# Linear attention and a squared-ReLU block with fast matrix products: the last weight pieces asked for ahead of W_out's stores, and the opening's units in another order

## The chip, the cores and the metric

The kernel runs on one core of one Trainium2 chip. The metric is the device time in microseconds (us) of one execution. Before the change the median of three runs is 915.18 us (915.45, 915.18, 912.42). A core has five engines that work at the same time and wait for one another through semaphores: TensorE (PE, with its weight loads shown as PEld), VectorE (DVE), ScalarE (ACT), GpSimd (POOL), and SyncE (SP), which here only issues DMAs. Each engine takes its instructions in the order in which the program lists them.

## The reference

```python
def _attn_ref(q, k, v, g_norm):                 # (8, 8, 576, 64) each
    kv = np.einsum('bhsd,bhse->bhde', k, v)
    out = np.einsum('bhsd,bhde->bhse', q, kv)
    rms = np.sqrt(np.mean(out * out, axis=-1, keepdims=True) + 1e-06)
    return (out / rms * g_norm).astype(np.float32)

def _moe_ref(x, w_in, w_out):                   # (4608, 512), (512, 2048), (2048, 512)
    h = x @ w_in
    r = np.maximum(h, 0.0)
    g = r * r
    return (g @ w_out).astype(np.float32)

def reference(**kwargs):
    ...
    x = np.ascontiguousarray(attn_out.transpose(0, 2, 1, 3)).reshape(B * S, H * D)
    return _moe_ref(x=x, **moe_kwargs)
```

Attention without softmax: per batch and head a 64 x 64 matrix kv is summed over the sequence, the queries are multiplied with it, and each row of 64 is divided by its root mean square. The result, 4608 tokens of 512 features, goes through a feed-forward block of width 2048 whose activation is the square of ReLU. The two weight matrices arrive as 64-bit floats, which the kernel gets as pairs of 32-bit words.

## The kernel before

**Units and strips.** The work on queries, keys and values is cut into units (b, p): batch b and pair p of heads, of which there are four (NP) per batch. The feed-forward block works on nine strips of 512 tokens (N_STRIP). Its two products are computed by Strassen-like schemes: a product of 2 x 2 blocks is made of seven block products (ORDER = 1, 2, 6, 5, 7, 3, 4) on sums of blocks. The first strip (s = 0) is special: its up product is plain (`up_first`, L745), because the weights arrive only then, and its down product (`down`, L842) takes the seven blocks of W_out, in the order 1, 2, 5, 6, 7, 3, 4. Blocks 1, 2 and 5 lie in SBUF, in three parts of the tile `w_in` (`w_first`, L218); blocks 6, 7, 3 and 4 are fetched from the DRAM tile `w_out` by `stream` (L798) into tiles `w_blk`. Each block is also cut a second time: `deep_sums` (L885) makes four sums of its quarters in a tile `w_t`, and `store_deep_sums` (L828) stores them to `w_deep` for the later strips. `w_blk` and `w_t` share one pool of four buffers.

**Weight pieces.** Each matrix arrives in 16 pieces of 512 KB (`load_piece`, L227, into eight buffers `raw`); pieces 0 to 15 are W_in, 16 to 31 W_out. A piece is converted to 32-bit floats in two steps on ACT (`convert_on_act`, L238: tiles `w_c` and `raw`) and four on DVE (`conversion`, L248). `convert_pieces` (L265) does a pair of pieces, has ACT work up to two pieces ahead, and asks for further pieces at its end (`load_more`, L274). The second half of W_out's pieces (24 to 31) goes through `sums_out` (L300): conversion, block sums (L280), and four stores of 256 KB for each pair (L313). `store_first(b)` (L319, L321) stores one of the three parts kept in SBUF, in two DMAs of 512 KB.

**The order.** The whole order is written out by hand. The opening is the list `slices` from L623 to L628: T is `transposed_query` (four PE transposes and a copy on ACT), K is `key_value` (products of keys and values on PE, two copies into `kv_all` on ACT), Q is `first_queries` (products with the queries, then ACT's squares and DVE's means), N is `first_normalized` (a root on ACT, then DVE, tile `x_n`), F is `first_features` (transposes of x_n on PE, copy on ACT), `act` and `piece` are the steps of a conversion on ACT and on DVE, and U is `first_up`, the first products of the up part. `keep_busy(ps, n)` (L360) lets PE multiply the identity matrix n times into a PSUM tile that is overwritten later.

After the opening, the loop at L1189 goes through the steps i of strip 0: 16 steps of `up_first` (n_up = 16) and 14 of `down`. Around each step stand the calls of `convert`, which emit the conversions; `attend`, which emits the next entries of `slices` (units of batch 1, then the features of strip 1); and the loads. Units are loaded in a fixed order by `load_next` (L174): it is called with steps 0, 1 and n_up + 8, and after the keys of units (1, 0) and (1, 1), which asks for (1, 3) and (2, 0):

```python
            if b < 2:
                if b == 1 and p < 2:
                    load_next()
```

All these DMAs, stores too, are issued by SP and so stand in one queue, in the order in which the program lists them.

Of the kernel before, what the change touches and what calls it, by code (L numbers as in the profile page):

```python
# [10 lines left out]
FP32 = mybir.dt.float32  # L11
# [9 lines left out]
def kernel(  # L21
# [35 lines left out]
    P = 128  # L57
# [6 lines left out]
    C = S // P  # L64
# [4 lines left out]
    NT = 4  # L69
# [104 lines left out]
    def load_next(q_eng=nc.sync, names="kvq"):  # L174
        u = next(to_load, None)
        if u is not None:
            load(*u, q_eng, names)
# [141 lines left out]
    def store_first(b):  # L319
        for e in range(2):  # L320
            nc.sync.dma_start(out=w_out[b, :, e], in_=w_first[b][:, :, ts(e, P)])  # L321
# [38 lines left out]
    def keep_busy(ps, n):  # L360


        for _ in range(n):
            nc.tensor.matmul(ps, lhsT=ident, rhs=ident[:, : ps.shape[1]], start=True, stop=True)
# [34 lines left out]
    def key_value(b, *ps_of):  # L399
        while any(f == load and a[:2] == (b, p) or f == load_rest and a[0] == b for _, f, a in keys_due for p in ps_of):  # L400
            _, f, a = keys_due.popleft()
            f(*a)
        ps = apsum.tile([P, len(ps_of), D], FP32, name="kv_ps", tag="at")
        for i, p in enumerate(ps_of):
            tk, tv = main.pop(("k", b, p)), main.pop(("v", b, p))
            if (b, p) == (0, 0):
                keep_busy(ps[:, 0], 3)
            half = slice(REST * (b % 2), REST * (b % 2 + 1))
            for c in range(C + 1):
                for h in range(2):  # L410
                    a, w = (t[:, h, c, :] if c < C else r[half, 2 * p + h] for t, r in ((tk, k_rest), (tv, v_rest)))
                    nc.tensor.matmul(ps[ts(h, D), i], lhsT=a, rhs=w, start=c == 0, stop=c == C)  # L412
        at = (NP * b + ps_of[0]) % (2 * NP)
        d = kv_all[:, at : at + len(ps_of)]
        nc.scalar.copy(d[0:D, :, 0:D], ps[0:D])
        nc.scalar.copy(d[D:P, :, D:P], ps[D:P])
        for i, p in enumerate(ps_of):
            kvd[b, p] = d[:, i]
            if b < 2:
                if b == 1 and p < 2:  # L420
                    load_next()
            else:
                u = next(to_load, None)
                if u is not None:
                    keys_later(load, *u, nc.sync, "kv")
                if p == NP - 1 and b + 1 < B:
                    keys_later(load_rest, b + 1, nc.sync)
# [88 lines left out]
    first = {}  # L516
# [100 lines left out]
    slices, ready = [], {}  # L617
# [2 lines left out]
        convert_on_act, transposed_query, key_value, first_queries, first_normalized, first_features, first_piece  # L620
    )
    U = first_up
    slices += [(T, (0, 0)), (K, (0, 0)), (Q, (0,)), (T, (0, 1)), (K, (0, 1)), (N, (0,)), (Q, (1,)), (act, (0,))]  # L623
    slices += [(T, (0, 2)), (F, (0,)), (K, (0, 2)), (piece, (0, 2)), (N, (1,)), (Q, (2,)), (act, (1,)), (piece, (0, 2))]
    slices += [(T, (0, 3)), (F, (1,)), (K, (0, 3)), (U, (0, [0])), (piece, (1, 2)), (N, (2,)), (Q, (3,)), (act, (2,))]
    slices += [(piece, (1, 2)), (U, (0, [1, 2])), (piece, (2, 1)), (N, (3,)), (act, (3,)), (F, (2,)), (U, (1, [0]))]
    slices += [(piece, (2, 3)), (F, (3,)), (piece, (3, 4))]
    slices += [(U, (1, [1, 2])), (U, (2, [0, 1, 2])), (U, (3, [0, 1, 2]))]  # L628
    ready[0] = len(slices)
    def query_pairs(b):  # L630
# [534 lines left out]
    for s in range(N_STRIP):  # L1165
        attend(ready[s])
        if s == DEEP_UP - 1:
            while queried:
                attend(slice_at[0] + 1)
            psums.close()  # L1170
            fpsum = ctx.enter_context(tc.tile_pool(name="fpsum", bufs=5, space=bass.MemoryType.PSUM, reuse_waits="tile"))
            apsum = ctx.enter_context(tc.tile_pool(name="apsum", bufs=1, space=bass.MemoryType.PSUM, reuse_waits="tile"))
        if s >= DEEP_UP:
            steps = [(0.5, up_slot, (s, slot)) for slot in range(55)]
        elif s == 0:
            steps = [(2, up_first, (g, fh, i)) for g in range(NG) for fh in range(2) for i in range(2)]
        else:
            steps = [(1, up, (s, g, p)) for g in range(NG) for p in ORDER]
        n_up = len(steps)
        if s < DEEP:  # L1180

            steps += [(2, down, (s, p, i)) for p in (ORDER if s else (1, 2, 5, 6, 7, 3, 4)) for i in range(2)]
        else:
            steps += [(2, down_deep, (s, k, i)) for k in range(7) for i in range(2)]
        goal, begun = ready.get(s + 1, len(slices)), slice_at[0]
        if s >= DEEP_UP:
            goal = max(goal, min(ready[DEEP_UP] + (len(slices) - ready[DEEP_UP]) * (s - 1) // (N_STRIP - DEEP_UP - 1), len(slices)))
        total, done = sum(w for w, _, _ in steps), 0
        for i, (w, fn, a) in enumerate(steps):  # L1189
            if s == 0 and i < n_up:  # L1190

                if 4 <= i < 10:
                    convert(3 + i)
                if i == 0:
                    load_next()
                    load_rest(1, nc.sync)
                    load_next()
                if i == 1:
                    load_next()
                if i == 2:  # L1200
                    for b in range(2):
                        load_q_rest(b, nc.sync)
                if i in (12, 13):
                    store_first(i - 12)
            elif s == 0 and i == n_up:
                convert(len(conversions))
                conv.close()
                store_first(2)

                stream_pool = ctx.enter_context(tc.tile_pool(name="stream", bufs=4, reuse_waits="tile"))  # L1210
                sum_pool = ctx.enter_context(tc.tile_pool(name="sum", bufs=8, reuse_waits="tile"))
            if s == 0 and n_up <= i < n_up + 2:
                for g in range(2 * (i - n_up), 2 * (i - n_up) + 2):
                    sum_g1(0, g)
            if s == 0 and n_up + 2 <= i < n_up + 4:
                for g in range(2 * (i - n_up) - 4, 2 * (i - n_up) - 2):
                    sum_g3(0, g)
            fn(*a)
            if s == 0 and i < 4:

                convert(3 + i)
            done += w
            if s:
                clock[0] += 3.2 if i >= n_up else 2.2 if s == DEEP else 1.2
                soon = tiles_due and tiles_due[0][2][0] // NT == s + 1
                if i == n_up + 10:
                    while tiles_due and tiles_due[0][2][0] // NT == s + 1:
                        _, f, a = tiles_due.popleft()
                        f(*a)
                elif not due(keys_due) and not (soon and due(tiles_due)):  # L1230
                    least = 2.1 if s == DEEP else 4.5 if i < n_up else 3.3
                    if not (n_up * 2 // 3 < i < n_up + 3) and clock[0] >= dripped[0] + least:
                        dripped[0] = clock[0]
                        drip(True)
                pace = 25 if s == DEEP else 36
                attend(begun + (goal - begun) * min(i + 1, pace) // pace)
                if s == DEEP and i == n_up - 3:
                    leaf_sums(s, 4)
                if s == 1 and i in range(2, 23, 3):
                    deep_sums_in((1, 6, 5, 4, 0, 2, 3)[i // 3])  # L1240
                if s == 1 and i in (21, 22, 23, 25):
                    stream()
                continue
            if i == n_up + 1:
                stream()
            if i == n_up + 8:
                load_next()
            if i == n_up + 9:
                load_rest(2, nc.sync)
                load_q_rest(2, nc.sync)  # L1250
            if i - n_up in (7, 8, 9, 12):
                sums_in((7, 8, 9, 12).index(i - n_up))
            if i == n_up + 11:
                sums_x(1)
            n = i + 1 - (n_up - 6)
            pairs, m = divmod(max(n - 2 * NP, 0), 3)
            attend(min(ready[0] + min(max(n, 0), 2 * NP) + (n >= 2 * NP) + 4 * pairs + (0, 2, 2)[m], goal))
            while deep_due and i != n_up + 1:
                store_deep_sums(*deep_due.popleft())
            if 11 <= i < n_up:  # L1260

                convert((13, 13, 14, 15, 16)[i - 11])
# [30 lines left out]
```

## Time and profile before

| | |
|---|---|
| median of three runs | 915.18 us |
| profiled execution: its time, its span from first to last instruction | 915.83 us, 913.7 us |
| mean granted TensorE clock | 0.99 |
| PE busy | 887.0 us (97% of the span) |
| PEld, DVE busy | 827.8 us (91%), 734.1 us (80%) |
| ACT, POOL busy | 315.0 us (34%), 306.4 us (34%) |
| DMA | 235.71 MB, mean 258 GB/s |

The profile is of one execution. Its time holds some 2 us that lie outside the span. Busy time is an average over stages that differ: in the first 180 us PE is busy 162 us, DVE 147 and ACT 92. In a timeline line the first two numbers are start and duration in us, then the engine, the line, the operation, the tiles written and read, the shape and the count; in brackets stands the idle time of the engine in front of it and what ended that. "SPq" is SP's queue, where the duration is that of issuing. In a list of waits the numbers are us in total, how many, and the longest.

### The profile page before, as it was taken

The page shows a single profiled execution, that of the slowest core. Times are in us where ns is not written, and L with a number is a line of the kernel's source. Part 1 is how long each engine was busy: PE and PEld are TensorE (multiplying, and loading weights), DVE is VectorE, ACT ScalarE, POOL GpSimd, SP SyncE. Part 2 cuts the span into 40 slices and gives each one's busy share as a digit, 9 for nine tenths or more (in the row PEclk, how much of TensorE's full clock was granted, in tenths as well). Part 3 has the DMA queues.
Part 4 walks back from the last instruction along what each step waited for, and adds up shares of the span by engine and source line. Part 5 has one row for each costly group of instructions (what it writes and reads, how often), then busy time and mean ns, then how long its engine had stood idle before and what let it go on. Part 6 is the DMA issues. An engine that isn't in the chain of part 4 may idle for free.

```text
span 913.7 us, 20581 instructions
## 1 busy us (share of the span) xinstructions
PE 887.0 (97%) x8246; PEld 827.8 (91%) x8246; DVE 734.1 (80%) x1256; ACT 315.0 (34%) x622; POOL 306.4 (34%) x315
## 2 busy tenths in 40 slices
PE   7899699999999999999999999999999999999998
PEld 7445578889999999999999998999999999999998
DVE  2999699678868895789688967887689868975886
ACT  4797342321024601370137011720263027202710
POOL 0000002910157504660456044514262347244700
PEclk7999899999999999999999999999999999999999
DMA  9998997999978797989877888879656866685385
GB/s 273 303 319 239 262 338 218 266 278 335 302 244 234 246 325 252 234 257 338 259 216 221 327 293 204 262 266 325 201 157 267 298 215 195 254 305 177 121 316 179
DMA packets 172367, 235.71 MB, mean 258 GB/s; under 512 B 83568, under 2 KB 137328, under 8 KB 163824
## 3 DMA queue, kind: packets, MB, share of 16 engines
q1 hardware_dynamic: 172112, 234.40, 80.4%
q8 instruction: 65, 1.06, 0.5%
q14 instruction: 30, 0.25, 0.1%
q10 hardware_dynamic: 160, 0.00, 0.0%
HBM read 197.66 MB, written 36.70 MB: 256 GB/s over the span
## 4 chain that ended last, share of the span: by engine, by line
PE 81%; DVE 9%; DMA 5%; SPq 2%; issue 2%; POOL 1%; ACT 1%; DVEq 0%; ACTq 0%
PE ps_B L927 20%; PE ps_A L1115 16%; PE ps_A L927 15%; PE ps_B L1115 8%; PE ps_A L712 4%; PE ps_C L1115 4%; PE kv_ps L412 2%; PE ps_A L753 2%; PE ps_B L712 2%; DMA w_blk<-w_deep 2%; PE ps_C L753 2%; PE x_ps L446 1%; PE ps_B L753 1%; DVE o_sb L942 1%; DVE gt L1127 1%
## 5 line engine op out<-in xcount | busy, mean ns | idle before, releaser
L927 PE MATMUL ps_B<-w_blk,g_s 128*128 128x128 f32 x1024 | 126.3, 275 | 0.0
L927 PEld LDWEIGHTS ps_B<-w_blk,g_s 128*128 128x128 f32 x1024 | 120.0, 192 | 0.2
L1115 PE MATMUL ps_A<-x_l,w_in 128*128 128x128 f32 x784 | 104.1, 276 | 0.0
L280 POOL TENSOR_TENSOR x_l<-xT 128x256 f32<-128x256 f32 x21 | 15.4, 733 | 248.1 <-PE ps_A L927 248.1
L927 PE MATMUL ps_B<-w_blk,gt 128*128 128x128 f32 x768 | 97.5, 275 | 0.1
L1115 PEld LDWEIGHTS ps_A<-x_l,w_in 128*128 128x128 f32 x784 | 95.4, 192 | 0.5 <-DVE gt L1127 0.2
L927 PE MATMUL ps_A<-w_blk,g_s 128*128 128x128 f32 x768 | 93.6, 275 | 0.0
L927 PEld LDWEIGHTS ps_B<-w_blk,gt 128*128 128x128 f32 x768 | 91.5, 192 | 0.4 <-DMA w_blk<-w_deep 0.3
L927 PEld LDWEIGHTS ps_A<-w_blk,g_s 128*128 128x128 f32 x768 | 89.6, 192 | 0.0
L1127 POOL TENSOR_TENSOR snap<-snap,gt 128x512 f32<-128x512 f32 x35 | 46.6, 1330 | 123.0 <-ACT snap L1132 57.6
L1132 ACT COPY snap<-ps_A 128x512 f32<-128x512 f32 x63 | 36.6, 582 | 132.3 <-PE ps_A L1115 119.4
L942 DVE TENSOR_TENSOR o_sb<-o_sb,ps_B 128x256 f32<-128x256 f32 (+1 forms) x128 | 49.4, 386 | 34.6 <-ACT o_sb L943 27.3
L1065 ACT ACTIVATE gt<-gt 128x512 f32<-128x512 f32 x112 | 69.7, 622 | 18.0 <-DVE gt L1127 17.9
L927 PE MATMUL ps_A<-w_blk,gt 128*128 128x128 f32 x576 | 72.3, 275 | 1.3 <-DMA w_blk<-w_deep 1.3
L1066 ACT ACTIVATE gt<-gt 128x512 f32<-128x512 f32 x112 | 70.6, 630 | 3.6
L927 PEld LDWEIGHTS ps_A<-w_blk,gt 128*128 128x128 f32 x576 | 68.2, 192 | 1.5 <-DMA w_blk<-w_deep 1.5
L1025 POOL TENSOR_TENSOR w_i<-w_in 128x512 f32<-128x512 f32 x7 | 9.6, 1365 | 154.2 <-ACT o_sb L874 152.9
L1127 POOL TENSOR_TENSOR gt<-gt,snap 128x512 f32<-128x512 f32 x42 | 52.5, 1276 | 24.7 <-DVE snap L1127 24.7
L280 DVE TENSOR_TENSOR gt<-gt 128x2048 f32<-128x2048 f32 (+1 forms) x29 | 59.7, 2063 | 0.0
L943 ACT COPY o_sb<-ps_A 128x128 f32<-128x128 f32 x24 | 6.4, 265 | 147.3 <-PE ps_A L927 147.3
L1115 PE MATMUL ps_A<-x_l,w_blk 128*128 128x128 f32 x392 | 52.3, 276 | 1.4 <-issue 1.2
L1115 PE MATMUL ps_B<-x_l,w_blk 128*128 128x128 f32 x392 | 52.0, 276 | 0.0
(176 smaller groups left out, 1820.1 us busy)
## 6 DMA issues: line engine op xcount, KB each, us to landing
w_blk<-w_deep SPq DMA_DIRECT2D x56, 1024.0 KB, 6.8
w_blk<-w_out SPq DMA_DIRECT2D x56, 768.0 KB, 5.9
w_blk<-w_in_deep SPq DMA_DIRECT2D x49, 768.0 KB, 5.1
raw<-in_moe_w_in_dram SPq DMA_DIRECT2D x16, 512.0 KB, 6.8
raw<-in_moe_w_out_dram SPq DMA_DIRECT2D x16, 512.0 KB, 6.6
k<-in_k_dram SPq DMA_DIRECT2D x29, 256.0 KB, 4.8
v<-in_v_dram SPq DMA_DIRECT2D x29, 256.0 KB, 5.1
x_d<-x_q SPq DMA_DIRECT2D x27, 256.0 KB, 5.3
```

Of the source, the lines that this page charges most:

```text
L280: eng.tensor_tensor(out=out, in0=a, in1=b, op=ALU.subtract)
L412: nc.tensor.matmul(ps[ts(h, D), i], lhsT=a, rhs=w, start=c == 0, stop=c == C)
L712: nc.tensor.matmul(bank[BANK[p]][:, i, :], lhsT=lhsT(k), rhs=rhs(k), start=p in (1, 5, 2) and i == 0 and k == 0, stop=k == n - 1, skip_gro ...
L753: nc.tensor.matmul(ps, lhsT=w_in[:, kc % KH, g, kc // KH * 2 + fh, ts(i, P)], rhs=xt[0][:, :, kc, :], start=kc == 0, stop=kc == NP - 1,)
L927: nc.tensor.matmul(chain[c][x][:, i, :], lhsT=a[:, f, :], rhs=w[:, f, :], start=x not in opened[c] and f == 0, stop=f == FQ // 2 - 1, skip ...
L942: add = lambda out, a, b: nc.vector.tensor_tensor(out=out, in0=a, in1=b, op=ALU.add)
L1025: nc.gpsimd.tensor_tensor(out=s1, in0=w_half(b, 0, 1), in1=w_half(b, 1, 1), op=ALU.add)
L1065: nc.scalar.activation(o, o, AF.Relu)
L1066: nc.scalar.activation(o, o, AF.Square)
L1115: nc.tensor.matmul(ps[:, i, :], lhsT=w, rhs=rhs, start=j in (1, 2, 5) and i == 0, stop=True, skip_group_check=True)
L1127: add = lambda eng, out, a, b: eng.tensor_tensor(out=out, in0=a, in1=b, op=ALU.add)
L1132: nc.scalar.copy(t, ps)
```

## The change

The change edits three places.

- `key_value`: for the first unit the identity products ahead of the keys are five instead of three, and four more, into a new PSUM tile of the tag "first", are put between the products of the whole rows and those of the 64 rest rows.
- `slices`: in the opening the transposes of unit (0, 1) stand ahead of the query products of unit 0, those of unit 2 ahead of the products of unit 1, and so on; the DVE steps of a piece are called four at once for pieces 0 and 1; the products U of the first feature block are called one by one.
- The loop over the steps of strip 0 and `key_value`: the first two of W_out's kept parts are no longer stored at steps 12 and 13 but with the third, at step n_up, behind all conversions; and unit (2, 0) is no longer loaded after the keys of (1, 1) but behind these stores.

```diff
--- before.py
+++ after.py
@@ -404,9 +404,12 @@
         for i, p in enumerate(ps_of):
             tk, tv = main.pop(("k", b, p)), main.pop(("v", b, p))
             if (b, p) == (0, 0):
-                keep_busy(ps[:, 0], 3)
+                keep_busy(ps[:, 0], 5)
+                warm = apsum.tile([P, NT, P], FP32, name="x_ps", tag="first")[:, 0]
             half = slice(REST * (b % 2), REST * (b % 2 + 1))
             for c in range(C + 1):
+                if (b, p, c) == (0, 0, C):
+                    keep_busy(warm, 4)
                 for h in range(2):
                     a, w = (t[:, h, c, :] if c < C else r[half, 2 * p + h] for t, r in ((tk, k_rest), (tv, v_rest)))
                     nc.tensor.matmul(ps[ts(h, D), i], lhsT=a, rhs=w, start=c == 0, stop=c == C)
@@ -417,7 +420,7 @@
         for i, p in enumerate(ps_of):
             kvd[b, p] = d[:, i]
             if b < 2:
-                if b == 1 and p < 2:
+                if b == 1 and p == 0:
                     load_next()
             else:
                 u = next(to_load, None)
@@ -620,11 +623,11 @@
         convert_on_act, transposed_query, key_value, first_queries, first_normalized, first_features, first_piece
     )
     U = first_up
-    slices += [(T, (0, 0)), (K, (0, 0)), (Q, (0,)), (T, (0, 1)), (K, (0, 1)), (N, (0,)), (Q, (1,)), (act, (0,))]
-    slices += [(T, (0, 2)), (F, (0,)), (K, (0, 2)), (piece, (0, 2)), (N, (1,)), (Q, (2,)), (act, (1,)), (piece, (0, 2))]
-    slices += [(T, (0, 3)), (F, (1,)), (K, (0, 3)), (U, (0, [0])), (piece, (1, 2)), (N, (2,)), (Q, (3,)), (act, (2,))]
-    slices += [(piece, (1, 2)), (U, (0, [1, 2])), (piece, (2, 1)), (N, (3,)), (act, (3,)), (F, (2,)), (U, (1, [0]))]
-    slices += [(piece, (2, 3)), (F, (3,)), (piece, (3, 4))]
+    slices += [(T, (0, 0)), (K, (0, 0)), (T, (0, 1)), (Q, (0,)), (K, (0, 1)), (N, (0,)), (T, (0, 2)), (Q, (1,))]
+    slices += [(act, (0,)), (F, (0,)), (K, (0, 2)), (piece, (0, 4)), (N, (1,)), (T, (0, 3)), (Q, (2,)), (act, (1,))]
+    slices += [(F, (1,)), (U, (0, [0])), (K, (0, 3)), (piece, (1, 4)), (N, (2,)), (U, (0, [1])), (Q, (3,)), (act, (2,))]
+    slices += [(F, (2,)), (U, (0, [2])), (piece, (2, 2)), (N, (3,)), (act, (3,)), (U, (1, [0])), (piece, (2, 2))]
+    slices += [(F, (3,)), (piece, (3, 4))]
     slices += [(U, (1, [1, 2])), (U, (2, [0, 1, 2])), (U, (3, [0, 1, 2]))]
     ready[0] = len(slices)
     def query_pairs(b):
@@ -1200,12 +1203,12 @@
                 if i == 2:
                     for b in range(2):
                         load_q_rest(b, nc.sync)
-                if i in (12, 13):
-                    store_first(i - 12)
             elif s == 0 and i == n_up:
                 convert(len(conversions))
                 conv.close()
-                store_first(2)
+                for b in range(3):
+                    store_first(b)
+                load_next()
 
                 stream_pool = ctx.enter_context(tc.tile_pool(name="stream", bufs=4, reuse_waits="tile"))
                 sum_pool = ctx.enter_context(tc.tile_pool(name="sum", bufs=8, reuse_waits="tile"))
```

## The prediction

> **What bounds the kernel now.** I read first the page's busy row: TensorE (PE) is busy 97% of the span, so a gain must come from its idle time or from half-clock time. Next the waits, 84 to 104 us: one wait of 8.2 us is nearly all the idle time that PE has after the opening.
>
> ```profile
> ACT w_c L242 <- DMA raw<-in_moe_w_out_dram: 13.8, 2, 13.6
> DVE w_c L254 <- ACT w_c L242: 8.6, 2, 7.5
> PE kv_ps L412 <- ACT kv_all L416: 8.2, 1, 8.2
> ```
>
> ScalarE (ACT) stands 13.6 us in front of weight piece 30; VectorE (DVE) waits for its output, and PE for the copies (kv_all) queued behind it. Why the piece is late stands in the timeline of SP's queue (start, duration):
>
> ```profile
> 79.41 3.45 SPq L313 DMA_DIRECT2D w_out<-wt  x4
> 82.92 4.65 SPq L321 DMA_DIRECT2D w_out<-w_in  x4
> 87.67 1.75 SPq L130 DMA_DIRECT2D k<-in_k_dram  x1
> ...
> 93.77 1.46 SPq L230 DMA_DIRECT2D raw<-in_moe_w_out_dram  x2
> 95.33 14.29 SPq L313 DMA_DIRECT2D w_out<-wt  x12
> 109.67 1.33 SPq L321 DMA_DIRECT2D w_out<-w_in  x2
> 112.02 0.42 SPq L807 DMA_DIRECT2D w_blk<-w_out  x1
> 117.50 2.85 SPq L840 DMA_DIRECT2D w_deep<-w_t  x2
> ```
>
> Pieces 30 and 31 (93.77) are asked for behind four stores of W_out (L321) and six loads of unit (2,0). What must be kept for the change: w_blk (112.02, block 6) stands behind the last stores, and w_deep (117.50) behind it. Then the timelines of PE and DVE:
>
> ```profile
> 103.64 1.12 PE L412 MATMUL kv_ps<-v,k 128*64 128x64 f32 x16 [8.20 <-ACT kv_all L416]
> ...
> 132.45 1.22 PE L574 MATMUL xt_ps<-ident,x_n 128*128 128x128 f32 x8 [1.70 <-DVE x_n L514]
> ```
>
> ```profile
> 100.12 0.43 DVE L254 TENSOR_SCALAR w_c<-w_c 128x512 f32<-128x512 f32 x1 [7.53 <-ACT w_c L242]
> ...
> 124.14 0.68 DVE L280 TENSOR_TENSOR w_t<-w_in 128x512 f32<-128x512 f32 x1
> ...
> 131.61 1.29 DVE L514 TENSOR_TENSOR x_n<-x_ps,newton 128x512 f32<-128x512 f32 x2
> ```
>
> Between these two places DVE has no gap: PE's next wait, 1.70 us at 132.45, is for DVE. Last, the windows (PE, weight loads, DVE, ACT, POOL, granted clock, DMA share, GB/s):
>
> ```profile
> 10.00:15.00 5.00, 4.48 (x34) 3.84 (x34) 1.08 (x4) 1.80 (x5) 0.00 (x0) 0.50 0.89 273
> ...
> 84.00:92.00 8.00, 8.00 (x49) 5.45 (x48) 8.00 (x22) 1.81 (x5) 0.00 (x0) 1.00 1.02 270
> 92.00:96.00 4.00, 3.44 (x16) 2.68 (x15) 0.59 (x2) 0.00 (x0) 0.00 (x0) 1.00 1.14 224
> 109.00:112.00 3.00, 3.00 (x17) 2.66 (x16) 2.97 (x6) 0.40 (x2) 0.00 (x0) 1.00 1.15 346
> 116.00:122.00 6.00, 6.00 (x34) 5.33 (x33) 5.96 (x11) 1.07 (x2) 0.00 (x0) 1.00 0.93 391
> ```
>
> The DMA engines are full: 270 GB/s while W_out's parts are stored, 224 in (2,0)'s loads, 346 for L313, 391 for w_blk and w_deep.
>
> **What the Trainium skill says.** "TensorE: Matmul & The Clock Gate", Part 1 on the clock gate: an idle window of about 3.4 us halves the clock until a window is busy. The trace agrees: 0.66 granted in 100 to 110, after the 8.2 us. The same page, "Engine queue depths", calls ACT and DVE strict first-in-first-out: the 13.6 us above is this. Its Part 4 says that transposes do not count as PE-busy; the clock of 0.50 at 10 to 15, with PE busy 4.48 of 5 us, partly with transposes, fits it and doesn't prove it. "DMA: Bandwidth & Descriptors", "Queues, rings and completion order": on each DMA engine descriptors are consumed in ring order. The landings seen here follow the order of issue, so what SP asks for first delays what comes after.
>
> **Stores: what goes.** In the changed order SP reaches piece 30 once the L313 stores are issued, at 82.86, and its buffer is free when piece 26 is converted, about 82.9. With the 5.6 us to landing of the issue at 93.77 it lands near 88.6, piece 31 near 90. ACT, free at 85.9, does both pieces by 91.1 (four operations of 0.66) and the copies by 92.6; PE needs them at 95.45 and DVE needs piece 30 at 92.6. So PE's 8.2 us and DVE's gaps (7.53 + 1.04, less overlap, 8.75) are gone. DVE ends the last sums at 99.0 instead of 107.77. PE would reach block 6 (123.57 before) at 113.7: 8.2 us less, and 1.7 us of half clock.
>
> **Stores: what comes.** After the last L313 stores SP now has six stores of 512 KB (3072 KB) and the six loads (768 KB) ahead of w_blk; before, two stores. L313's four last stores move from 99.65 to 102.7 (1024 KB at 346). Six stores at 275 KB/us (the first seconds of L321, as 270 GB/s): 11.2 us, to 113.9; (2,0)'s loads, 768 KB at 224: 3.4, to 117.3; w_blk, 1 MB at 391: 2.6, and about 0.7 to its landing: 120.6. PE waits from 113.7 to 120.6, so 6.9 us of its gain of 9.9 are lost at once, and some 2.3 us more at half clock (estimate from the 1.7 paid now, with denser work).
>
> Next late is DVE. The sums of block 5 (124.14 above) go into the buffer from which block 1's sums were stored: the program of the kernel before gives both the same address, and the first instruction waits for that store. The store is w_deep's first, right behind w_blk: 2.6 us more, landing near 123.2 (121.3 before, where DVE came at 124.14 and found it done). DVE reaches that instruction at 115.6 now, and waits 7.6 us. From it to x_n and PE's products took 132.45 - 124.14 = 8.3 us in one unbroken line of DVE, so PE goes on at 131.5 instead of 132.45. This hides the half clock of block 6 (done near 129.7). Sum of this part: -0.95 us, as DVE's -8.77 is met by +7.8 of queue. From there on all is as before; block 7's w_blk lands 7.5 us after w_deep, at 130.7, in time for 132.6.
>
> **Opening.** Two more identity products in front of keys (4 of about 0.11 us) lie in the 0.64 us wait for v; four at 128 columns (8 of 0.107) in the 0.93 us wait for v_rest: nothing, and 0.1 if the cover is short. They may hold the clock at 8.6. Transposes of unit 1 ahead of Q(0): its q, issued at 5.36, lands after the median 4.1 at 9.4, before 9.64: Q(0) is 0.3 to 0.7 later, covered, since unit 2 is awaited. The transposes of unit 2 stand ahead of Q(1) and need q issued at 8.46 with 6.5 to landing: 14.9, so Q(1) starts at 15.4, not 14.52, and ends at 17.4, where it ended at 16.59. Its means on DVE start at 18.2 (17.27 before). Whole conversions take back what this loses: DVE has the same work, and its 1.2 us gap before 20.16, waiting for the root, fills with piece 0. Counting 12.3 us of DVE work from 18.2 and 0.8 of waits, x_n of unit 3 comes at 31.25 against 30.83. At full clock throughout Q(1) ends 1 us earlier and it comes at 30.3. The end of that chain feeds ACT's relu at 36.80, then DVE: -0.5 to +0.9 us, I take +0.35. The loads of (1,3) stay; those of (2,0), wanted only after 150, cost nothing but the place counted above.
>
> **Sum.** -0.95 + 0.35 = -0.6 us. The profiled execution took 915.83 (span 913.7 and 2.1 around it): 915.2. The median shown, 915.18, is 0.65 lower: 914.6.
>
> **Rivals.**
> - DVE is not held by the buffer: then PE is bound by w_blk alone, 120.6 + 2.3 of half clock, and keeps about 2.4 us, with a warm opening 3: 911.9. For it: the clocks of the opening; against: the address.
> - The full gain: w_blk lands by 114 to 116, 7 to 9.5 us, 906.5. It needs 4.9 MB in 12 us, 410 KB/us; 512-byte store packets show 270 to 346.
> - Slower: the queue runs slower still. If the 3840 KB of stores and loads move at 224 throughout, they take 17.1 us, not 14.6, and DVE's wait and all behind grow by 2.5; with an opening at +0.9 the end is +2.5 to +3.2: 918. It decides from a landing of w_deep 1 us later than I put it.
> - The change doesn't do what it says: piece 30 still lands past 95 (another wait holds SP). Then the 8.2 us stay and the queue's +7.8 comes on top: 923.
>
> **Chances and range.** Forecast 0.52 (its own range 912.5 to 917.5), DVE not held 0.19, full gain 0.08, slower queue 0.14, not as said 0.07. Range 909.0 to 919.0: it takes in the first and third rival and both ends of the opening. About 0.3% (2.75 us) is what a measurement here can tell: faster is the full gain, most of the DVE rival and the forecast's edge, 0.26; slower 0.22; same 0.52.
>
> **What would show it.** PE's wait at 103.64 gone and K at 95.5; a PE wait for w_blk of 6 to 7 us before block 6 and clock 0.5 after it; a DVE wait of 7 to 8 us at w_t for the store w_deep; PE's transposes of x_n near 131.5. If w_t doesn't wait, or w_blk lands before 117, I am too slow; if x_n of unit 3 comes past 32 or piece 30 past 92, too fast.

## The result and the profile after

The change makes the kernel slower: 918.75 us (median of six runs, 916.9 to 920.69) against 913.89 for the kernel before (six runs, 912.18 to 915.45). The ratio of the two times is 1.0053, with a 95% interval of 1.0032 to 1.0074. The forecast was 914.6.

The two profiled executions show less of it: 917.25 us after (span 915.3), 915.83 before (span 913.7). The kernel before was thus drawn 1.9 us above its median, the changed one 1.5 below. What sets a single execution apart is a main finding below.

Below, a transfer "lands" when the trace reports it done, and "unit 3" is the last unit of the opening, (0, 3). First the list of waits after, 84 to 126 us (us in total, times, longest):

```profile
DVE w_t L280 <- DMA w_deep<-w_t: 11.1, 1, 11.1
...
PE ps_A L715 <- DMA w_blk<-w_out: 10.8, 1, 10.8
...
ACT w_c L242 <- DMA raw<-in_moe_w_out_dram: 2.9, 1, 2.9
```

PE's 8.2 us for kv_all are gone, and of ACT's 13.6 for piece 30 2.9 are left. In their place stand 10.8 us of PE for block 6's w_blk and 11.1 of VectorE (DVE) for w_deep's first store. SP's queue after, with the start and the length of issuing, says why both are late:

```profile
81.11 0.92 SPq L230 DMA_DIRECT2D raw<-in_moe_w_out_dram  x2
84.03 15.03 SPq L313 DMA_DIRECT2D w_out<-wt  x12
99.10 8.28 SPq L321 DMA_DIRECT2D w_out<-w_in  x6
107.48 1.77 SPq L130 DMA_DIRECT2D k<-in_k_dram  x1
...
110.63 3.02 SPq L121 DMA_DIRECT2D q<-in_q_dram  x4
113.70 2.10 SPq L810 DMA_DIRECT2D w_blk<-w_out  x1
115.90 0.85 SPq L843 DMA_DIRECT2D w_deep<-w_t  x2
```

Pieces 30 and 31 are asked for at 81.11 instead of 93.77. The six stores and unit (2,0)'s six loads now stand ahead of w_blk (113.70; 112.02 before) and w_deep. The timelines of PE and DVE after:

```profile
93.28 0.69 PE L415 MATMUL kv_ps<-v,k 128*64 128x64 f32 x16
...
122.45 9.56 PE L715 MATMUL ps_A<-w_blk,gt 128*128 128x256 f32 x32 [10.82 <-DMA w_blk<-w_out]
133.12 1.22 PE L577 MATMUL xt_ps<-ident,x_n 128*128 128x128 f32 x8 [1.11 <-DVE x_n L517]
```

```profile
96.45 0.75 DVE L280 TENSOR_TENSOR wt<-w_in,wt 128x256 f32<-128x256 f32 x2
...
124.79 0.69 DVE L280 TENSOR_TENSOR w_t<-w_in 128x512 f32<-128x512 f32 x1 [11.14 <-DMA w_deep<-w_t]
...
132.28 1.29 DVE L517 TENSOR_TENSOR x_n<-x_ps,newton 128x512 f32<-128x512 f32 x2
```

Keys start at 93.28 instead of 103.64, and DVE's last block sum ends at 97.20 instead of 107.77: 10 us are won there, 1.8 of them in the opening. At the transposes of x_n (133.12, before 132.45) nothing is left of them. The windows after (PE, weight loads, DVE, ACT, POOL, granted clock, DMA share, GB/s):

```profile
92.00:97.00 5.00, 5.00 (x100) 4.22 (x99) 5.00 (x13) 2.09 (x5) 0.00 (x0) 1.00 0.58 172
97.00:113.00 16.00, 14.64 (x133) 12.68 (x131) 15.69 (x31) 3.44 (x7) 0.00 (x0) 1.00 0.99 274
113.00:117.00 4.00, 0.00 (x0) 0.00 (x0) 0.66 (x2) 0.00 (x0) 0.00 (x0) 0.59 0.85 174
117.00:122.00 5.00, 0.00 (x0) 0.00 (x0) 0.00 (x0) 0.00 (x0) 0.00 (x0) 0.50 0.90 272
122.00:127.00 5.00, 4.55 (x11) 3.68 (x12) 2.17 (x4) 0.00 (x0) 0.00 (x0) 0.50 1.01 426
```

From 92 to 97, ahead of the six stores, the DMA has room (share 0.58, 172 GB/s). From 113 to 122 PE does nothing and DVE 0.66 us. Full DMA engines mean little by themselves: they moved 174 GB/s at 113 to 117, where the queue passes from q's small packets to w_blk, and 426 at 122 to 127.

### The profile page after: what moved, and what is told of

The parts are those of the page before. It is cut to its first block, busy times and chain, and to the rows that moved or that the text cites. A ratio compares the mean times of both kernels' runs of the same rounds, so it can differ in the third digit from the quotient of the medians.

```text
span 915.3 us, 20607 instructions
## 1 busy us (share of the span) xinstructions
PE 885.2 (97%) x8258; PEld 825.8 (90%) x8258; DVE 734.2 (80%) x1256; ACT 315.3 (34%) x622; POOL 306.4 (33%) x315
## 4 chain that ended last, share of the span: by engine, by line
PE 80%; DVE 8%; DMA 5%; SPq 3%; ACT 3%; issue 2%; DVEq 0%; ACTq 0%
PE ps_B L930 21%; PE ps_A L1118 18%; PE ps_A L930 15%; PE ps_B L1118 9%; PE ps_C L1118 4%; PE ps_A L715 4%; PE kv_ps L415 2%; PE ps_B L715 2%; DMA w_blk<-w_deep 2%; PE x_ps L449 2%; DMA w_deep<-w_t 1%; DVE w_c L260 1%; SPq L321 1%; DVE wt L280 1%; ACT raw L245 1%
## 5 line engine op out<-in xcount | busy, mean ns | idle before, releaser
L1068 ACT ACTIVATE gt<-gt 128x512 f32<-128x512 f32 x112 | 69.7, 622 | 18.2 <-DVE gt L1130 18.1
```

Of the source, the lines that this page charges most:

```text
L1068: nc.scalar.activation(o, o, AF.Relu)
```

## The experiments

Each run stands against runs of the kernel before on the same chip; their medians lie between 913.9 and 914.5 us, and at 915.58 for the last timed run, so between groups of runs the ratios compare, not the medians.

**The change again, and its two parts.** `after_again` is the change unaltered. `stores_only` is the kernel before with its third edit alone (the stores behind all conversions, unit (2,0) behind them), `opening_only` the kernel before with the two others.

> The changed kernel once more, for a second trace and more times. Its first trace is 1.6 us longer than that of before, its median 4.9 us. Theory Q (the queue of six stores and six loads between the last L313 store and w_deep's landing is what costs): near +4.9 us again, with w_deep's first landing 27 us or more after DVE's last sum (27.6 in the first trace, 24.2 in my forecast), and the rest of the difference in later waits for DMAs. Theory O (the other order of the opening costs): +4.9 too, with x_n of the fourth unit later than 30.8, where the first trace has it at 29.0.

> Before with the stores' part of the change alone: W_out's kept parts and unit (2,0) behind all conversions, the opening as before. Theory Q: slower than the whole change by the 1.9 us that the opening gained in the trace, some 920 (+6 to +7 us against before); DVE's last sum near 99, the wait of w_t for w_deep 10 to 11 us. Theory O: no slower than before, 912 to 914.

> Before with the opening's part alone, stores and loads where they were. Theory Q: 1 to 2 us faster than before (x_n of the fourth unit 1.9 us earlier), with the 8 us wait for weight piece 30 still there, some 912. Theory O: slower by 4 to 5 us, 918.

Measured: the change 918.92 us (ratio 1.0061, interval 1.0044 to 1.0078), the stores alone 915.96 (1.0025; 1.0014 to 1.0035), the opening alone 915.55 (1.0017; 1.0006 to 1.0027). Both parts lose. Neither time is what the theories had: for the stores alone they had some 920 and 912 to 914, for the opening alone 912 and 918. The sum of the parts, 0.42%, lies below the 0.61% of the whole here and just outside its interval; the table of terms below shows what the parts do to each other.

**Which of the two late transfers sets the end.** `q_mid` puts (2,0)'s loads between w_blk and w_deep; `own_buffer` gives block 5's deep sums tiles of their own, so that DVE need not wait for w_deep's store.

```diff
 # q_mid: the change with
-                load_next()          # at step n_up, behind the stores
             if i == n_up + 1:
                 stream()
+                load_next()          # behind block 6's w_blk
 # own_buffer: the change with
-        if p == 6:
+        if p in (5, 6):              # store_deep_sums: four tiles of sum_pool
-        if s == 0 and p in (2, 6, 3):
-            reserve({2: 5, 6: 7, 3: 4}[p])
+        if s == 0 and p in (6, 3):
+            reserve({6: 7, 3: 4}[p])
```

> The change, with the six loads of unit (2,0) moved from ahead of block 6's w_blk to just behind it, so that they stay ahead of the two w_deep stores. If PE's wait for w_blk ends last (theory W): w_blk lands 4 to 5 us earlier, near 117.5, and the time falls by as much, to some 914.5. If DVE's wait for the buffer that w_deep's store leaves ends last (theory B): w_blk lands as early, PE's wait moves from w_blk to x_n, and the time is that of the change within 1 us, some 918.5.

> The change, with one thing different: the deep sums of block 5 get a buffer that W_out's store w_deep doesn't read, so VectorE need not wait for that store at the half of its sums w_t. The queue is as in the change. Theory B (this wait ends last): the wait of 11 us at w_t is gone, the wait of 1 to 2 us of TensorE's transposes for x_n is gone too, and TensorE is bound by w_blk and the half clock after it: 1 to 2 us faster than the change, 917 to 918. Theory W (TensorE's wait for w_blk alone sets the end): nothing changes, 918.8. If the buffer were the whole matter: 7 us faster, 912.

`q_mid` took 918.62 us (1.0052; 1.0033 to 1.0072), as the change. PE's timeline in it:

```profile
119.64 8.96 PE L715 MATMUL ps_A<-w_blk,gt 128*128 128x256 f32 x32 [5.50 <-DMA w_blk<-w_out]
133.33 1.73 PE L577 MATMUL xt_ps<-ident,x_n 128*128 128x128 f32 x8 [4.73 <-DVE x_n L517]
```

PE's wait for w_blk is halved, and what it wins is lost again at x_n. So it is DVE's wait that ends last. In `own_buffer` DVE does not wait; it took 917.11 us (1.0027; 1.0012 to 1.0042), 1.8 us below `after_again` by the medians and 3.1 by the ratios, and PE's timeline has no wait before x_n any more:

```profile
124.00 9.21 PE L715 MATMUL ps_A<-w_blk,gt 128*128 128x256 f32 x32 [10.29 <-DMA w_blk<-w_out]
133.04 1.04 PE L577 MATMUL xt_ps<-ident,x_n 128*128 128x128 f32 x8
```

The two waits lie nearly level: taking away the later one is worth only what stands between it and the next.

**The queue.** `q_late` puts (2,0)'s loads behind block 7's w_blk, so that both w_blk and w_deep follow the stores at once. `spread` does this and puts two of the three groups of stores where the DMA has room: behind pieces 30 and 31, but before the end of the L313 stores. `spread_old` is the same with the opening of the kernel before.

```diff
 # q_late: the change with load_next() moved from step n_up to
+            if i == n_up + 3:
+                load_next()
 # spread: also
+                if i in (14, 15):
+                    store_first(i - 14)
             elif s == 0 and i == n_up:
-                for b in range(3):
-                    store_first(b)
+                store_first(2)
```

> The change, with the six loads of unit (2,0) moved behind block 7's w_blk, so that block 6's w_blk and the store w_deep follow the six stores at once. Both land about 5 us earlier (3.8 us of loads and the 1.5 us in which the DMA stood nearly idle behind them). Theory Q (the queue between the last L313 store and w_deep is what eats the gain): TensorE's wait for w_blk falls from 10.8 to about 6, VectorE's from 11 to about 6, and the time falls by 4 to 5.5 us, to 913 to 915. If the end is set elsewhere (the opening, or a later wait for unit (2,0)): within 1 us of 918.8.

> As the one before, and the first two groups of stores of W_out are asked for two steps apart behind weight pieces 30 and 31, where the DMA has room, rather than all three at the end. Theory Q: w_blk lands before TensorE comes for it (no wait, no half clock), VectorE finds its buffer free, and the 8.2 us of the wait removed are kept: 905 to 909. If the stores only push L313's back: 911 to 915. If the opening has cost most of the loss: above 912.

> The same order of stores and loads with the opening of the kernel before. Against the run with the new opening: theory O (the new opening costs 1 to 2 us in any company, as it does alone, 1.6): 1 to 2 us faster than that run, 904 to 908. If the new opening's loss was hidden or was chance: the same within 0.7 us. If it gains where the stores' part is in order: slower by up to 1 us.

`q_late` took 914.06 us (1.0002; 0.9985 to 1.0019), 4.7 below the change; PE's timeline:

```profile
117.68 9.45 PE L715 MATMUL ps_A<-w_blk,gt 128*128 128x256 f32 x32 [5.84 <-DMA w_blk<-w_out]
128.42 1.23 PE L577 MATMUL xt_ps<-ident,x_n 128*128 128x128 f32 x8 [1.29 <-DVE x_n L517]
```

`spread` took 909.8 (0.9942; 0.9925 to 0.9959), 0.8 us above what was expected, `spread_old` 906.33 (0.9926; 0.9902 to 0.9950). By the medians the old opening is 3.5 us faster there, by the ratios 1.5, and the intervals overlap. In `spread` PE finds w_blk there:

```profile
113.88 7.17 PE L715 MATMUL ps_A<-w_blk,gt 128*128 128x256 f32 x32
124.21 1.94 PE L577 MATMUL xt_ps<-ident,x_n 128*128 128x128 f32 x8 [3.16 <-DVE x_n L517]
```

The queue behind the stores is the cause of the stores' loss: with the stores spread, asking early for pieces 30 and 31 gains 6.8 us (by the ratio) to 8.1 us (by the medians) in the old opening, most or all of the 8.2 us of the wait removed.

**The opening, with the stores spread.** `q1_first` puts unit 1's query products back ahead of unit 2's transposes in `spread`; `q1_halves` also cuts the conversions into halves again; `no_ident` is `spread` with three identity products as before; `ident_only` is `spread_old` with the change's identity products.

```diff
 # q1_first: spread with
-... (N, (0,)), (T, (0, 2)), (Q, (1,))]
+... (N, (0,)), (Q, (1,)), (T, (0, 2))]
 # q1_halves: q1_first with each of pieces 0 and 1 as, e.g.,
-(piece, (0, 4)), (N, (1,)), (T, (0, 3)), (Q, (2,)), (act, (1,)), (F, (1,))
+(piece, (0, 2)), (N, (1,)), (T, (0, 3)), (Q, (2,)), (act, (1,)), (piece, (0, 2)), (F, (1,))
```

> On the run with the stores spread (909.8 with the change's opening, 906.3 with the old one): the change's opening, with unit 1's query products put back ahead of the transposes of unit 2. Theory T (TensorE stands at those transposes for unit 2's q, 2.1 to 2.5 us, with Q(1) behind them, and the idle window gives a half clock at 14): VectorE's reduction of unit 1's means starts near 15.7 instead of 18.1, x_n of unit 3 near 28.4 instead of 30.6, no half clock at 14 to 18, and the time falls by 2 to 3.5 us to 906.5 to 908. Theory P (the whole pieces put ahead of the means cost it): x_n of unit 3 moves by under 1 us, and the time stays above 909.

> As the first of these, with each weight piece converted in halves around the means and root as in the kernel before. Theory P (whole conversions delay the means' newton steps on VectorE): 0.5 to 1.5 us below the first of these. If the whole conversions only fill waits: the same within 0.7 us.

> The run with the stores spread and the change's opening, without its added identity products (three ahead of keys as before, none in the second wait). Theory C (these products keep TensorE's clock full at 8 to 12 in every execution): the half clock comes back at about 9, x_n of unit 3 at 31 or later, and the time is 1 to 2 us above 909.8. If they do nothing: the same within 0.7.

> The old opening with the stores spread, plus the change's identity products alone (two more ahead of keys, four ahead of the rest's products). If they hold the clock at 8 to 12 and cost nothing: no half clock before 14, x_n of unit 3 at 27.6 to 28.3 in the trace, and the time 0 to 1.5 us below the 906.3 of the same kernel without them. If they delay the first units: 0.3 to 1 us above it.

`q1_first` took 908.83 us (0.9949; 0.9927 to 0.9971): x_n of unit 3 came 1.9 us earlier in the trace, as theory T has it, but the time does not differ from `spread` (0.9942), where theory T had 2 to 3.5 us. `no_ident` took 908.22 (0.9936; 0.9914 to 0.9959) and `ident_only` 906.93 (0.9930; 0.9904 to 0.9955): no time gained or lost by the identity products is seen, and theory C's forecast for `no_ident` (a half clock at about 9, 1 to 2 us more) did not come. `q1_halves` took 913.05 (0.9989; 0.9969 to 1.0008), 4.2 slower than `q1_first` where theory P expected it faster: PE now waits 3.3 us for converted weights (w_in) in the opening. Theory P fell.

**The opening, edit by edit in the kernel before.** `t2_ahead` moves only T(0,2) ahead of Q(1), `ident_before` adds only the identity products, `whole_only` only makes the conversions whole; `after_q1` is the change with Q(1) put back ahead of T(0,2).

```diff
 # t2_ahead: the kernel before with
-... (N, (0,)), (Q, (1,)), (act, (0,)), (T, (0, 2)), (F, (0,)), ...
+... (N, (0,)), (T, (0, 2)), (Q, (1,)), (act, (0,)), (F, (0,)), ...
 # whole_only: the kernel before with
-... (piece, (0, 2)), (N, (1,)), (Q, (2,)), (act, (1,)), (piece, (0, 2)), ...
+... (piece, (0, 4)), (N, (1,)), (Q, (2,)), (act, (1,)), ...
 # and so for piece 1; piece 2 in two and two steps instead of one and three
```

> The kernel before, with only one step of the opening moved: the transposes of unit 2 ahead of unit 1's query products, as the change has them. Theory T (this step is what the opening loses): TensorE waits 2 us or more there for unit 2's q, VectorE's second reduction starts near 18, x_n of unit 3 comes 1.5 to 2.5 us later than in the kernel before at the same clock, and the time is 1.5 to 2.5 us above 913.9. If another part of the opening costs it: within 0.7 us of 913.9.

> The kernel before with the change's identity products alone. Theory C (they hold the clock at 8 to 12 and nothing is late for them): no half clock ahead of 20, x_n of unit 3 near 27.6 to 28.3 where the cold execution had it at 30.1, and, as only part of the executions are cold, 0.5 to 1.5 us below 913.9. If they cost more than they hide: above 914.5.

> The kernel before with only the conversions of weight pieces 0 to 2 made whole ahead of the means' newton steps, in the old order. Theory P (a whole piece is 2.2 us of VectorE where the wait for the root is 1.0): units 1 and 2 are 0.5 to 1 us late each, but the halves behind them are gone, so x_n of unit 3 moves by 0 to 1 us: 913.9 to 915. If they fill waits that are there: 913 to 914.

> The change, with unit 1's query products put back ahead of the transposes of unit 2. Theory T carried through: the opening's 1.6 us come back, 916.5 to 917.5. If the stores' queue sets the end whenever the opening ends, since w_deep's landing is counted from the last stores and not from VectorE: within 0.7 us of 918.8.

| | median, us | ratio to before | interval |
|---|---|---|---|
| t2_ahead | 915.12 | 1.0006 | 0.9990 to 1.0021 |
| ident_before | 913.64 | 0.9995 | 0.9983 to 1.0007 |
| whole_only | 912.33 | 0.9981 | 0.9969 to 0.9992 |
| after_q1 | 916.90 | 1.0032 | 1.0020 to 1.0044 |

`whole_only` is faster than either case that was expected of it (913 to 915). `after_q1` gives back 1.9 us of the change, about what the opening costs alone. By itself the same step is inconclusive (`t2_ahead`). PE's timelines show where PE stands. First the opening of the change (`opening_only`), then of `t2_ahead`, then of `after_q1`:

```profile
15.06 1.09 PE L388 MATMUL t_ps<-ident,first_qkv 128*128 128x128 f32 x4 [2.53 <-DMA first_qkv<-in_q_dram]
15.94 1.92 PE L527 MATMUL x_ps<-kv_all,qT 128*128 128x128 f32 x8
```

```profile
14.72 0.63 PE L388 MATMUL t_ps<-ident,first_qkv 128*128 128x128 f32 x4 [0.71 <-ACT rms L469]
```

```profile
12.92 1.16 PE L527 MATMUL x_ps<-kv_all,qT 128*128 128x128 f32 x8 [0.52 <-ACT kv_all L419]
14.27 0.63 PE L388 MATMUL t_ps<-ident,first_qkv 128*128 128x128 f32 x4 [0.19 <-DMA first_qkv<-in_q_dram]
```

In the change PE is through with unit 1's keys at 12.5 and stands 2.5 us at unit 2's q, with Q(1), which needs no such load, behind it. In `t2_ahead` the keys end only at 14.0, behind a half clock from 9.8 to 13.2, and unit 2's q landed at 14.58, so that little of the wait is left. What the step costs at full clock this trace does not show: in `stores_only`, whose opening ran at full clock in the old order, these keys end at 12.1.

The landing of unit 2's second q accounts for most of what sets the traces of the new opening apart. SP issues it at 8.45 to 8.55 us in the seven traces with the change's opening (the change, `after_again`, `opening_only`, `q_mid`, `own_buffer`, `q_late`, `spread`), and it lands between 13.43 and 14.92. Where no half clock follows, x_n of unit 3 starts 14.9 us after that landing (28.32, 28.56 and 29.17 for landings at 13.43, 13.67 and 14.27); where one does, 15.6 to 16.2 us after it. In `stores_only` the q landed at 14.39 and x_n started at 27.56. My estimate from these figures: with that landing the change's opening would have brought x_n at 29.3 at full clock, 1.7 us later, about what `opening_only` loses.

Making the conversions whole gains 1.6 us in the kernel before. If that gain holds in the changed opening too, the new order by itself loses some 3.2 us (1.6 + 1.6); this was not measured.

**The base, and the best version.** `before_b` is the kernel before once more, for a second trace; `spread_whole` is `spread_old` with `whole_only`'s edit.

> The kernel before, once more, for a second trace of it. If the first profiled execution was a slow one because its half clock in the opening lasted 10.2 us: here the half clock lasts 3.4 us or less, x_n of unit 3 starts at 27.5 to 28.5 instead of 30.1, TensorE's transposes of x_n at 100 to 140 start near 130 instead of 132.45, and the time is 912 to 914. If long half clocks are the rule: as the first, 915 to 916.

> The best parts together: the stores spread, the old order of the opening without new identity products, and the conversions whole. If the gain of the whole conversions (1.6 us alone) adds to that of the spread stores (906.3): 904 to 905.5. If it goes into later waits, as part of the gains at x_n of unit 3 did with the stores spread: 905.5 to 907.

`spread_whole` took 906.0 us against 915.58 (0.9891; 0.9867 to 0.9914), some 9.6 us faster than the kernel before. Its interval and that of `spread_old` (0.9902 to 0.9950) still overlap, so that the whole conversions add here is likely, not shown.

`before_b` took 912.87 us. One window, 8 to 20 us, of the first trace of the kernel before, then of `before_b`, then of `stores_only`, whose opening is the same code:

```profile
8.00:20.00 12.00, 9.78 (x73) 8.48 (x73) 3.86 (x11) 5.48 (x15) 0.00 (x0) 0.57 1.02 322
```

```profile
8.00:20.00 12.00, 9.73 (x82) 8.65 (x83) 4.64 (x16) 5.52 (x16) 0.00 (x0) 0.72 1.05 340
```

```profile
8.00:20.00 12.00, 8.31 (x94) 6.88 (x96) 6.04 (x19) 6.98 (x18) 0.00 (x0) 1.00 1.00 319
```

The granted clock is 0.57, 0.72 and 1.00, for 10.2, 6.8 and 0 us at half. x_n of unit 3 starts at 30.14, 29.01 and 27.56; `spread_old`, with 3.4 us at half clock, lies between, at 28.35. So the same program moves by up to 2.6 us with the half clock of its opening. My expectation of 3.4 us or less for `before_b` was wrong, its time as expected.

The traces then add up in four terms, each read from timelines as above: the start of x_n of unit 3; from there to the end of DVE's last block sum (wt); from there to its first sum of block 5 (w_t); and 8.3 us to PE's transposes of x_n.

| | x_n of unit 3 | to the last wt | to w_t | PE's x_n | time of that execution |
|---|---|---|---|---|---|
| before | 30.14 | 77.63 | 16.37 | 132.45 | 915.83 |
| before_b | 29.01 | 76.94 | 16.38 | 130.65 | 912.87 |
| opening_only | 31.09 | 76.96 | 16.4 | 132.75 | 916.23 |
| stores_only | 27.56 | 68.89 | 25.97 | 130.74 | 913.59 |
| the change | 28.32 | 68.88 | 27.59 | 133.12 | 917.25 |
| after_again | 29.17 | 68.87 | 27.29 | 133.66 | 917.00 |
| after_q1 | 27.92 | 68.86 | 27.56 | 132.66 | 915.21 |

From PE's x_n to the full time of the execution every row has 782.2 to 784.1 us. At an equal opening the stores' part wins 8.1 us in the second term (8.75 against the first trace) and loses 9.6 (`stores_only`) to 11.2 (the change) in the third: +1.5 us alone and +3.1 with the new opening. The 3.1 and the opening's own 1.6 come to 4.7, near the 4.9 measured.

## Why the prediction was wrong

**The bound and what goes** were right. Piece 30 landed at 86.6 (forecast 88.6), PE's wait vanished, keys came at 93.28 (95.5), and the last sum moved by 8.1 to 8.8 us against the opening (8.77).

**What comes, in kind:** right. PE waits for w_blk and pays half clock after it, DVE is held by the buffer w_deep's store reads, and this wait is the later one (`q_mid`, `own_buffer`). The line from w_t to x_n is 8.33 us (8.3). The rivals that DVE is not held and that nothing holds the gain are out, and so is that the change doesn't do what it says.

**What comes, in size:** the failed step. The sum from DVE's last block sum to w_deep's landing was 24.2 us; it measured 27.6 (97.20 to 124.77), 25.97 in `stores_only`. By its terms, forecast and landings of the trace after:

| | forecast, us | measured, us |
|---|---|---|
| to the end of the L313 stores | 3.7 | 4.2 (to 101.43) |
| six stores, 3072 KB | 11.2 | 11.85 (to 113.28) |
| loads of (2,0), 768 KB | 3.4 | 3.8 (to 117.05) |
| w_blk, 1 MB, and its landing | 3.3 | 5.3 (to 122.32) |
| w_deep | 2.6 | 2.45 (to 124.77) |

The rates of the stores and loads were nearly right. The largest miss is w_blk: I priced it at 391 KB/us from the moment the loads end, as if it were already in line. But SP's issue of it took until 115.80, and the DMA moved 52 and 89 KB in the two us from 115 and 116, then 240 to 250 KB/us before it reached 400. From the end of its issue to its landing w_blk took 6.5 us here, 6.0 to 6.3 in `after_again`, `after_q1` and `own_buffer`, and 5.9 in `stores_only`. What differs is that end: it came 2.5 to 3.0 us behind the last store's landing in those four and 1.3 in `stores_only`, where the issue took 0.85 us instead of 2.10 and w_blk landed 7.3 us after the last store instead of 9.0. The late issue is thus most of why the change loses 1.6 us more in that term than the stores alone; that the small packets of q's loads hold up SP is argued from their place, and why `stores_only`, with the same order, escaped it stays open. In `stores_only` the loads (5.0 us) and w_blk (2.2) together are only 0.5 above the forecast 6.7; there the miss is spread over the terms, and the 8.77 us that were to be won were 8.1 at an equal opening.

This is the rival of the slower queue, in another place: it said 224 KB/us throughout the stores and loads, and a landing of w_deep 1 us later than forecast as the point from which it decides. Counted from the last sum it was 3.4 later; the early opening of that execution hid 1.8 of them. That this rival's 918 came near 918.75 is partly luck: the stores ran at 259 KB/us (3072 KB in 11.85 us), not at 224, and the opening lost more than it had.

**Opening:** the working holds for the execution that it was worked out for. Q(1) was to start at 15.4 and end at 17.4; it ran 15.94 to 17.86 in `opening_only`. Means on DVE were to start at 18.2 and did at 18.52, and x_n was to end at 31.25, and ended at 31.78. That the identity products cost nothing was right (`ident_before`), and that they may hold the clock at 8.6 is borne out by the traces, without a gain in time clear of noise (see the last section). That transposes on PE go with the half clock at 10 to 15 is not borne out: `stores_only` does the same transposes at full clock, so that they alone do not bring it. "Whole conversions take back what this loses" is right in direction: they gain 1.6 us alone. What failed is the base, and the landing of unit 2's q, which was taken as fixed at 14.9. 30.83 came from an execution with 10.2 us of half clock; the three other traces with that opening unaltered start x_n at 27.56 to 29.01 (30.14 in the first), while seven with the change's opening start it at 28.3 to 31.1, four of them with 3.4 us of half clock that begins between 14.1 and 15.5, in or right behind the wait for unit 2's q. So +0.35 us was +1.6 (`opening_only`). I set the full-clock case at 30.3 and took it as the better end of the changed kernel; but the old opening runs at full clock too (`stores_only`), and then 2.6 us ahead of the first trace.

**Sum.** -0.95 becomes +2.0 (stores) and +0.35 becomes +1.6 (opening), together +3.6 where the whole measured +4.9. The interval of the first measurement (2.9 to 6.8) holds 3.6, that of `after_again` (4.0 to 7.1) does not; the 1.6 us by which w_deep, counted from DVE's last sum, lands later in the change than in `stores_only` are a likely source of the rest. One slip of the working: DVE's two gaps shown add up to 8.57 us, not 8.75, which alone would have moved the forecast by 0.2. The profiled time of before, from which the sum was made, lay 1.9 us above the median of the later runs; taking off the 0.65 to the three runs shown was too little.

## What to carry to other kernels

When a request is moved ahead of stores, add up the whole queue from the last store's source to the next buffer that a store must free, and ask of each transfer when its issue ends, not only when its forerunner ends: w_blk landed 5.9 to 6.5 us after the end of its issue in the five traces that put it right behind (2,0)'s loads. Stores that only need to be done before a later load belong where the DMA has room, two steps apart here (`spread`), not in one block ahead of that load. Before comparing two single traces line by line, compare the granted clock of each stage: a stage with many short waits can run at full or at half clock in two executions of the same program, and the difference is carried to the end. Compare the landings that it waits for as well.

## What the runs showed that was not expected

- Half-clock stretches last 3.41, 6.83, 10.24 or 13.65 us, whole multiples of 3.41 (but for the one that the end cuts off), and begin at another moment in each execution: in the kernel before at 8.6 and at 9.9, in `stores_only` not at all in the opening. The Trainium skill, "TensorE: Matmul & The Clock Gate", Part 1 on the clock gate, calls the window of about 3.4 us free-running, which agrees.
- One such window goes with 0.7 to 1.1 us of x_n in the old opening (27.56, 28.35, 29.01, 30.14 for none, one, two and three, one trace each).
- The half clock ahead of 14 us is not chance alone. Of the eight traces without the added identity products six have a half clock that begins between 8.6 and 10.2; of the twelve with them none has one before 14.1. Still `ident_before` gained nothing clear of noise (-1.6 to +0.6 us).
- The six stores of 512 KB took 11.8 to 11.9 us from the last L313 landing to their own last in five traces (`stores_only`, the change twice, `after_q1`, `own_buffer`), but block 6's w_blk landed 7.3 us after them in `stores_only` and 8.5 to 9.1 in the others.
- A load asked for at the same moment lands up to 1.5 us apart from one execution to the next (unit 2's q, 13.43 to 14.92 in seven traces). In the change's opening unit 1's keys end at 11.9 to 12.5 us and PE then stands 1.4 to 2.7 us at this load with other work behind it, with a half clock in or right behind the wait in four of the seven.
